# The last pair's V as stationary operand, and a result made in two banks, on two engines, by two queues

**Chip, cores, metric.** One core of one Trainium2 chip. The metric is the device time of one execution in microseconds (us), median of several runs. A matmul of TensorE has a stationary operand, which is loaded first (LDWEIGHTS in the profile), and a moving one; its result goes to a tile in PSUM, which the program allots in banks. SyncE starts the transfers. The granted clock is the share of TensorE's full clock that it got by the profile.

## The reference

A decode step for four sequences, the sum of an attention block and a feed-forward block over one normalized input:

```python
xn = layernorm(x)                                    # x: [4, 1, 512] bf16
q = xn @ wq                                          # 32 heads of 128
p = softmax(einsum("bhqd,bhkd->bhqk", q, k_cache) * 128 ** -0.5)
o = einsum("bhqk,bhkd->bhqd", p, v_cache)            # caches: [4, 32, 8192, 128] bf16
out = x + o_flat @ wo + (silu(xn @ w_gate) * (xn @ w_up)) @ w_down
```

K and V each have one tile of 2 MiB for each of 128 pairs (head, sequence), 512 MiB in all, read once. There is one query row for each, so all the arithmetic is small beside the reading.

## The kernel before

The loop goes over M = 128 pairs m = 4 h + b. Iteration i treats K of pair i and, LP = 4 iterations later, V of that pair. Loads go into nine slots through SyncE's queue; the last V is loaded in four parts. The parts that the change touches:

```python
psM = ... tile_pool(name="psM", bufs=2, space=PSUM)      # 8 banks in all: psS 2, psO 2, psM 2, psX 1, psY 1
psY = ... tile_pool(name="psY", bufs=1, space=PSUM)
yo_ps = psY.tile([B, D], f32)                            # the result: [4, 512]

def pv_chunk(m, k):        # probabilities stationary (4 columns), V moving (512 columns)
    mm(o_acc[h % 2][b * QB:b * QB + NV, :], pt[h][:, s * NV:(s + 1) * NV, 2 * (b * NTG + g)],
       v_tiles[m][:, k * 512:(k + 1) * 512], start=(k == 0))

def fin_1(h):              # the accumulator of a head, 128 x 512, to SBUF
    nc.scalar.copy(out=o_sb[:], in_=o_acc[h % 2][:])

def fin_2(h):              # fold and turn: o as a column of 128 for each b, f32
    for u in range(NV):
        mm(xps[:], o_sb[:, u * Dh:(u + 1) * Dh], ident_f[:, u:P:QB], start=(u == 0))
    nc.vector.tensor_tensor(out=otn[:, h, :], in0=xps[:], in1=rcp.pop(h)[:], op=ALU.mult)

def wo_mm(h):
    mm(yo_ps[0:B, :], otn[:, h, :], w[:, h % (H // 2), :], start=False)
# ... the loop: 16 pv_chunk for each V; fin_1 after the fourth V of a head, fin_2 one iteration later ...
nc.vector.tensor_copy(out=res[:], in_=yo_ps[0:B, :])
nc.sync.dma_start(out=out_flat[:, :], in_=res[:])
```

`mm` is a helper, so nearly all matmuls carry its line, L74, and are told apart by their tiles: `sps` are scores, `oacc` the products with V, `xps` the folded columns, `yo_ps` the result.

Of the kernel before, what the change touches and what calls it, by code (L numbers as in the profile page):

```python
# [8 lines left out]
dt = mybir.dt  # L9
# [6 lines left out]
def kernel(  # L16
# [13 lines left out]
    nc = tc.nc  # L30
    P = nc.NUM_PARTITIONS

    B, Sq, D = A_x.shape
    _, H, Sk, Dh = A_k_cache.shape
# [5 lines left out]
    M = B * H  # L40
    T = Sk // P
    QB = 32
    NQ = P // QB
    TG = 16
    NTG = T // TG
# [10 lines left out]
    out_flat = out.flatten_outer_dims()  # L56
# [5 lines left out]
    persist = ctx.enter_context(tc.tile_pool(name="persist", bufs=1))  # L62
# [2 lines left out]
    small = ctx.enter_context(tc.tile_pool(name="small", bufs=2))  # L65
    psS = ctx.enter_context(tc.tile_pool(name="psS", bufs=2, space=bass.MemoryType.PSUM))
    psO = ctx.enter_context(tc.tile_pool(name="psO", bufs=1, space=bass.MemoryType.PSUM))
    psM = ctx.enter_context(tc.tile_pool(name="psM", bufs=2, space=bass.MemoryType.PSUM))
    psX = ctx.enter_context(tc.tile_pool(name="psX", bufs=1, space=bass.MemoryType.PSUM))
    psY = ctx.enter_context(tc.tile_pool(name="psY", bufs=1, space=bass.MemoryType.PSUM))  # L70
    ctx.enter_context(tc.manual_schedule())

    def mm(out_ap, lhsT, rhs, start, **kw):
        nc.tensor.matmul(out_ap, lhsT=lhsT, rhs=rhs, start=start, stop=True,  # L74
                         skip_group_check=True, **kw)
# [16 lines left out]
    k_tiles, v_tiles = {}, {}  # L92

    def load_k(m):
        h, b = divmod(m, B)
        t_ = slot()
        nc.sync.dma_start(out=t_[:], in_=A_k_cache[b, h, :, :].rearrange("(p t) d -> p (t d)", p=P))  # L97
        k_tiles[m] = t_

    def load_v(m, parts=1):  # L100
        h, b = divmod(m, B)
        t_ = slot()
        src = A_v_cache[b, h, :, :].rearrange("(p t) d -> p (t d)", p=P)
        w = SLOT // parts
        for i in range(parts):
            nc.sync.dma_start(out=t_[:, i * w:(i + 1) * w], in_=src[:, i * w:(i + 1) * w])
        v_tiles[m] = t_
# [7 lines left out]
    ident_f = const.tile([P, P], dt.float32, name="ident_f")  # L115
# [67 lines left out]
    for half in range(NH):  # L183
        for par in range(2):
            for x in range(8):
                mm(qt_ps[:, half, par, x, :], q_bf[:, half, par, x, :, :], pick,
                   start=(half == 0 and par == 0 and x == 0))
# [2 lines left out]

    yfx = persist.tile([B, D], dt.float32, name="yfx")
    otn = persist.tile([P, H, B], dt.bfloat16, name="otn")
    yo_ps = psY.tile([B, D], dt.float32, name="yo_ps")
    ffn = {}

    def load_ffn():
        wg_t, wu_t, wd_t = slot(), slot(), slot()
        w = EC * F
        nc.sync.dma_start(out=wg_t[:, 0:w], in_=B_w_gate.rearrange("(p c) f -> p (c f)", c=EC))
        nc.sync.dma_start(out=wu_t[:, 0:w], in_=B_w_up.rearrange("(p c) f -> p (c f)", c=EC))  # L200
        nc.sync.dma_start(out=wd_t[:, 0:FC * D], in_=B_w_down.rearrange("(p c) e -> p (c e)", c=FC))
        ffn["w"] = (wg_t[:, 0:w].rearrange("p (c f) -> p c f", c=EC),
                    wu_t[:, 0:w].rearrange("p (c f) -> p c f", c=EC),
                    wd_t[:, 0:FC * D].rearrange("p (c e) -> p c e", c=FC))

    def do_ffn():
        wg, wu, wd = ffn["w"]

        gu_ps = psM.tile([P, 2, FC * B], dt.float32, name="mps")
        for i, w in enumerate((wg, wu)):  # L210
            for fc in range(FC):
                for c in range(EC):
                    mm(gu_ps[:, i, fc * B:(fc + 1) * B], w[:, c, fc:F:FC], xnt_w[:, c, 0:B],
                       start=(i == 0 and fc == 0 and c == 0))
        eg = persist.tile([P, FC * B], dt.float32, name="eg")
        nc.scalar.activation(out=eg[:], in_=gu_ps[:, 0, :], func=ACT.Exp, scale=-1.0)
        nc.vector.tensor_scalar(out=eg[:], in0=eg[:], scalar1=1.0, scalar2=None, op0=ALU.add)
        sig = persist.tile([P, FC * B], dt.float32, name="sig")
        nc.vector.reciprocal(out=sig[:], in_=eg[:])
        gs = persist.tile([P, FC * B], dt.float32, name="gs")  # L220
        nc.vector.tensor_tensor(out=gs[:], in0=gu_ps[:, 0, :], in1=sig[:], op=ALU.mult)
        ht = persist.tile([P, FC * B], dt.bfloat16, name="ht")
        nc.vector.tensor_tensor(out=ht[:], in0=gs[:], in1=gu_ps[:, 1, :], op=ALU.mult)
        yf_ps = psM.tile([B, D], dt.float32, name="mps")
        for fc in range(FC):
            mm(yf_ps[0:B, :], ht[:, fc * B:(fc + 1) * B], wd[:, fc, :], start=(fc == 0))
        nc.vector.tensor_tensor(out=yfx[:], in0=yf_ps[0:B, :], in1=xf[:], op=ALU.add)  # L227

        mm(yo_ps[0:B, :], ident_f[0:B, 0:B], yfx[:], start=True)

    wo_t = []

    def load_wo(half):
        n = H // 2
        t_ = slot()
        nc.sync.dma_start(out=t_[:].rearrange("p (h e) -> p h e", h=n),
                          in_=A_wo[half * n * P:(half + 1) * n * P, :].rearrange("(h p) e -> p h e", p=P))
        wo_t.append(t_)


    kts, s_ps, pt, rcp, nmx, osb = {}, {}, {}, {}, {}, {}
# [9 lines left out]
    def t_piece(m, g):  # L251

        w = TG * Dh
        kt = kt_pool.tile([P, w], dt.bfloat16, name="kt")
        src = k_tiles[m][:, g * w:(g + 1) * w].bitcast(dt.uint32)
        nc.vector.transpose(out=kt[:].bitcast(dt.uint32).rearrange("p (j t r) -> p t j r", j=2, r=QB),  # L256
                            in_=src.rearrange("p (t j r) -> p t j r", j=2, r=QB))
        kts[m, g] = kt
# [11 lines left out]
    def max_1(h):  # L270
        mx = small.tile([P, 1], dt.float32, name="mx")
        nc.vector.reduce_max(out=mx[:], in_=s_ps[h][:], axis=AX.X)  # L272
        nmx[h] = mx
# [19 lines left out]
    def pt_turn(h):  # L293
        t_ = pp.tile([P, TG, QB], dt.bfloat16, name="pt_")
        nc.vector.transpose(out=t_[:].rearrange("p t x -> p (t x)"), in_=pt[h][:])
        pt[h] = t_
# [16 lines left out]
        nc.scalar.copy(out=o_sb[:], in_=o_acc[h % 2][:])  # L313
        osb[h] = o_sb

    def fin_2(h):

        o_sb = osb.pop(h)
        xps = psX.tile([P, B], dt.float32, name="xps")
        for u in range(NV):  # L320
            mm(xps[:], o_sb[:, u * Dh:(u + 1) * Dh], ident_f[:, u:P:QB], start=(u == 0))
        nc.vector.tensor_tensor(out=otn[:, h, :], in0=xps[:], in1=rcp.pop(h)[:], op=ALU.mult)  # L322

    def wo_mm(h):
        w = wo_t[h // (H // 2)][:].rearrange("p (h e) -> p h e", e=D)
        mm(yo_ps[0:B, :], otn[:, h, :], w[:, h % (H // 2), :], start=False)

    NK = T // NV
    R_FFN, R_WO = 8, M - 10
    wo_next, wo_ready = 0, 0  # L330
    build_q(0)
    for i in range(M + LP + 1):

        if i + 2 < M:
            load_k(i + 2)
        if 0 <= i + 2 - LP < M:
            load_v(i + 2 - LP, parts=4 if i + 2 - LP == M - 1 else 1)
        if i == R_FFN - 3:
            load_ffn()
        if i == R_FFN:  # L340
            do_ffn()
        if i == R_WO - 3:
            load_wo(0)
        if i == R_WO - 2:
            load_wo(1)
        hs, bs = divmod(i, B)
        hp = hs - 1
        if i < M:
            for g in range(NTG):
                t_piece(i, g)  # L350
                s_piece(i, g)
                if g == 0 and bs == 0 and hp >= 0:
                    pt_turn(hp)
            if bs == B - 2 and hs + 1 < H:
                build_q(hs + 1)
            if bs == B - 1:
                max_1(hs)
        elif i == M:
            pt_turn(H - 1)
        mp = i - LP  # L360
        if 0 <= mp < M:
            for k in range(NK):
                pv_chunk(mp, k)
                if k == NK // 2 and i < M and bs == B - 1:
                    max_2(hs)
            hv, bv = divmod(mp, B)
            if bv == 0:
                row_sums(hv)
            if bv == B - 1:
                fin_1(hv)  # L370
        elif i < M and bs == B - 1:
            max_2(hs)
        mf = i - LP - 1
        if 0 <= mf < M and mf % B == B - 1:
            fin_2(mf // B)
            wo_ready = mf // B + 1
        if i >= R_WO:
            for _ in range(5):
                if wo_next < wo_ready:
                    wo_mm(wo_next)  # L380
                    wo_next += 1
# [2 lines left out]
        wo_next += 1  # L384
    assert wo_next == H

    res = persist.tile([B, D], dt.bfloat16, name="res")
    nc.vector.tensor_copy(out=res[:], in_=yo_ps[0:B, :])  # L388
    nc.sync.dma_start(out=out_flat[:, :], in_=res[:])


# [28 lines left out]
```

## Time and profile before

| | before |
|---|---|
| time, median of the first 3 runs | 1297.76 us (1297.59 to 1297.80) |
| span in the trace | 1295.92 us |
| read from HBM | 550.77 MB, 425 GB/s over the span |
| DMA queue's share of the 16 engines | 99.6% |
| last V but one landed | 1284.17 us |
| from there to the end | 11.75 us |

The table is read from below: nearly everything is transfer, and what compute can change is the last row. The prediction shows the lines.

### The profile page before, as it was taken

The page shows a single profiled execution, that of the slowest core. Times are in us where ns is not written, and L with a number is a line of the kernel's source. Part 1 is how long each engine was busy: PE and PEld are TensorE (multiplying, and loading weights), DVE is VectorE, ACT ScalarE, POOL GpSimd, SP SyncE. Part 2 cuts the span into 40 slices and gives each one's busy share as a digit, 9 for nine tenths or more (in the row PEclk, how much of TensorE's full clock was granted, in tenths as well). Part 3 has the DMA queues.
Part 4 walks back from the last instruction along what each step waited for, and adds up shares of the span by engine and source line. Part 5 has one row for each costly group of instructions (what it writes and reads, how often), then busy time and mean ns, then how long its engine had stood idle before and what let it go on. Part 6 is the DMA issues. An engine that isn't in the chain of part 4 may idle for free.

```text
span 1295.9 us, 11245 instructions
## 1 busy us (share of the span) xinstructions
PE 1095.1 (85%) x4676; PEld 423.2 (33%) x4676; DVE 693.3 (54%) x887; ACT 48.5 (4%) x102; POOL 5.6 (0%) x11
## 2 busy tenths in 40 slices
PE   5889888888888888888888888888888888886987
PEld 2343333333333333333333333333333333332333
DVE  7635554554554565555565455555555555544542
ACT  1000000000000000000000000000000000000000
POOL 1000000000000000000000000000000000000000
PEclk8989999999999999999999999999989989998999
DMA  9999999999999999999999999999999999999997
GB/s 396 429 430 432 431 429 431 431 431 430 430 432 430 430 430 431 431 429 432 432 428 429 434 430 429 431 431 431 431 431 431 430 430 431 430 403 419 432 429 305
DMA packets 42210, 551.49 MB, mean 426 GB/s; under 512 B 4264, under 2 KB 8368, under 8 KB 8880
## 3 DMA queue, kind: packets, MB, share of 16 engines
q1 hardware_dynamic: 42160, 550.79, 99.6%
q8 instruction: 36, 0.59, 0.2%
q14 instruction: 14, 0.11, 0.0%
HBM read 550.77 MB, written 0.00 MB: 425 GB/s over the span
## 4 chain that ended last, share of the span: by engine, by line
DMA 91%; PE 5%; DVE 3%; issue 0%; SPq 0%; ACT 0%; DVEq 0%; ACTq 0%
DMA slot<-in_A_k_cache_dram 86%; DMA slot<-in_B_w_up_dram 3%; DVE kt L256 3%; DMA slot<-in_A_v_cache_dram 3%; PE oacc L74 2%; PE sps L74 2%; PE mps L74 1%; PE xps L74 0%; SPq L97 0%; PE mps L278 0%; SPq L89 0%; DVE mx L272 0%; DVE res L388 0%; DVE yfx L227 0%; ACT o_sb L313 0%
## 5 line engine op out<-in xcount | busy, mean ns | idle before, releaser
L256 DVE STREAM_TRANSPOSE kt<-slot 128x1024 uint32<-128x1024 uint32 x512 | 593.5, 1212 | 284.8 <-DMA slot<-in_A_k_cache_dram 284.8
L74 PE MATMUL sps<-kt,zq 128*128 128x512 bf16 x2048 | 572.1, 416 | 179.0 <-DVE kt L256 165.6
L74 PEld LDWEIGHTS <-zq 128*128 128x128 bf16 x2048 | 208.8, 103 | 532.0 <-issue 361.4
L302 DVE RECIPROCAL rcp<-mps 128x4 f32<-128x4 f32 x32 | 5.8, 183 | 160.9 <-PE mps L74 160.9
L272 DVE TENSOR_REDUCE mx<-sps 128x1 f32<-128x512 f32 x32 | 22.1, 692 | 45.1 <-PE sps L74 45.1
L281 DVE TENSOR_REDUCE nm<-mps 128x4 f32<-128x64 f32 x32 | 7.2, 225 | 50.0 <-PE mps L278 50.0
L74 PE MATMUL xps<-ident_f,o_sb 128*128 128x4 f32 x256 | 33.1, 253 | 0.7 <-ACT o_sb L313 0.7
L74 PEld LDWEIGHTS xps<-ident_f,o_sb 128*128 128x128 f32 x256 | 31.1, 192 | 1.2 <-ACT o_sb L313 1.2
L247 DVE COPY zq<-qt 32x16 bf16<-32x16 bf16 x128 | 23.5, 183 | 1.3
L322 DVE TENSOR_TENSOR otn<-xps,rcp 128x4 bf16<-128x4 f32 x32 | 5.2, 162 | 34.1 <-PE xps L74 34.1
L313 ACT COPY o_sb<-oacc 128x512 f32<-128x512 f32 x32 | 18.7, 585 | 20.6 <-PE oacc L74 20.5
L74 PE MATMUL oacc<-slot,pt__1952 128*4 128x512 bf16 x64 | 14.6, 379 | 0.0
L74 PE MATMUL oacc<-slot,pt__3394 128*4 128x512 bf16 x64 | 14.6, 379 | 0.0
L74 PE MATMUL oacc<-slot,pt__6498 128*4 128x512 bf16 x64 | 14.6, 379 | 0.0
L74 PE MATMUL oacc<-slot,pt__922 128*4 128x512 bf16 x64 | 14.6, 379 | 0.0
L74 PE MATMUL oacc<-slot,pt__2158 128*4 128x512 bf16 x64 | 14.6, 379 | 0.0
L74 PE MATMUL oacc<-slot,pt__3188 128*4 128x512 bf16 x64 | 14.6, 379 | 0.0
L74 PE MATMUL oacc<-slot,pt__4424 128*4 128x512 bf16 x64 | 14.6, 379 | 0.0
L74 PE MATMUL oacc<-slot,pt__5248 128*4 128x512 bf16 x64 | 14.6, 379 | 0.0
L74 PE MATMUL oacc<-slot,pt__6282 128*4 128x512 bf16 x64 | 14.6, 379 | 0.0
L74 PE MATMUL oacc<-slot,pt__371 128*4 128x512 bf16 x64 | 14.6, 379 | 0.0
L74 PE MATMUL oacc<-slot,pt__1128 128*4 128x512 bf16 x64 | 14.6, 379 | 0.0
(204 smaller groups left out, 636.8 us busy)
## 6 DMA issues: line engine op xcount, KB each, us to landing
slot<-in_A_k_cache_dram SPq DMA_DIRECT2D x128, 2048.0 KB, 38.4
slot<-in_A_v_cache_dram SPq DMA_DIRECT2D x127, 2048.0 KB, 38.8
slot<-in_A_wq_dram SPq DMA_DIRECT2D x2, 2048.0 KB, 9.4
slot<-in_A_wo_dram SPq DMA_DIRECT2D x2, 2048.0 KB, 28.8
slot<-in_A_v_cache_dram SPq DMA_DIRECT2D x4, 512.0 KB, 28.0
slot<-in_B_w_gate_dram SPq DMA_DIRECT2D x1, 1792.0 KB, 38.2
slot<-in_B_w_up_dram SPq DMA_DIRECT2D x1, 1792.0 KB
slot<-in_B_w_down_dram SPq DMA_DIRECT2D x1, 1792.0 KB, 34.0
```

The source lines that it names most:

```text
L74: nc.tensor.matmul(out_ap, lhsT=lhsT, rhs=rhs, start=start, stop=True, skip_group_check=True, **kw)
L247: nc.vector.tensor_copy(out=zq[h % 2][a * QB:(a + 1) * QB, :, :, XO + a * QB].rearrange("p b (j r) -> p r j b", r=2), in_=qt[a * QB:(a + 1 ...
L256: nc.vector.transpose(out=kt[:].bitcast(dt.uint32).rearrange("p (j t r) -> p t j r", j=2, r=QB), in_=src.rearrange("p (t j r) -> p t j r", ...
L272: nc.vector.reduce_max(out=mx[:], in_=s_ps[h][:], axis=AX.X)
L281: nc.vector.tensor_reduce(out=nm[:], in_=mps[:, 0:P].rearrange("p (a x g r) -> p x a g r", a=NQ, x=B, r=2)[:, :, :, :, 0], axis=AX.XY, op= ...
L302: nc.vector.reciprocal(out=r_[:], in_=mps[:, P:P + B])
L313: nc.scalar.copy(out=o_sb[:], in_=o_acc[h % 2][:])
L322: nc.vector.tensor_tensor(out=otn[:, h, :], in0=xps[:], in1=rcp.pop(h)[:], op=ALU.mult)
```

## The change

The intent is to shorten what follows the last transfers. For the last pair, V becomes the stationary operand: 64 pieces of 128 x 128 are loaded into the array and each is multiplied by one column of probabilities. (Below, "the 64 pairs" are these 64 weight loads, each with its matmul; "V 126" is V of the (head, sequence) pair 126.) So its o comes out as a column of `xps` at once, and the accumulator's copy and the fold are done for the other three sequences while V still arrives. The result is made in two banks so that two engines can cast it at the same time, and each half has its own store. The second bank comes out of `psM`, and with one `psM` buffer the feed-forward part must run an iteration later.

```diff
-    psM bufs=2 ... psY bufs=1
+    psM bufs=1 ... psY bufs=2
-    yo_ps = psY.tile([B, D], ...)
+    yo_ps = [psY.tile([B, DH], ...) for _ in range(2)]          # DH = 256; all matmuls into it: two of 256 columns
-    R_FFN, R_WO = 8, M - 10
+    R_FFN, R_WO = 9, M - 10
+    def fin_2(h, nb=B):                                         # folds the first nb columns, returns xps
+    def pv_last(xps):
+        h, b = divmod(M - 1, B)
+        for t in range(T):
+            g, u = divmod(t, TG)
+            mm(xps[:, b:b + 1], v_tiles[M - 1][:, t * Dh:(t + 1) * Dh],
+               pt[h][:, u, 2 * (b * NTG + g):2 * (b * NTG + g) + 1], start=False)
...
-        if 0 <= mp < M:
+        if mp == M - 1:
+            xps = fin_2(H - 1, B - 1)
+            pv_last(xps)
+            fin_3(H - 1, xps)                                   # the scaling that fin_2 did before
+            wo_ready = H
+        elif 0 <= mp < M:
...
-            if bv == B - 1:
+            if bv == B - 1 or mp == M - 2:
                 fin_1(hv)
...
-    nc.vector.tensor_copy(out=res[:], in_=yo_ps[0:B, :])
-    nc.sync.dma_start(out=out_flat[:, :], in_=res[:])
+    nc.vector.tensor_copy(out=res[0][:], in_=yo_ps[0][0:B, :])
+    nc.sync.dma_start(out=out_flat[:, 0:DH], in_=res[0][:])
+    nc.scalar.copy(out=res[1][:], in_=yo_ps[1][0:B, :])
+    nc.scalar.dma_start(out=out_flat[:, DH:D], in_=res[1][:])
```

## The prediction

> **What bounds the kernel now.** I first read the page's part on the DMA queues and the head of the chain that ended last, to learn whether an engine or the transfers set the 1297.76 us.
>
> ```profile
> DMA  9999999999999999999999999999999999999997
> q1 hardware_dynamic: 42160, 550.79, 99.6%
> DMA 91%; PE 5%; DVE 3%; issue 0%; SPq 0%; ACT 0%; DVEq 0%; ACTq 0%
> ```
>
> All 40 slices but the last are full of transfer, one queue keeps the 16 DMA engines busy for 99.6% of the span, and 91% of the chain is DMA. The kernel reads 550.77 MB at about 430 GB/s and nothing in the diff removes a byte of it. The TensorE's 85% busy is no bound: it waits for K and V. So only two short stretches can change the time: the start, before the transfers run full (untouched by the change), and the end, after the last of them lands. I therefore read the chain, in order of time, from 1280 us on (start, duration, what).
>
> ```profile
> 1251.39 32.78 DMA slot<-in_A_v_cache_dram
> 1284.17 0.04 issue
> 1284.21 6.23 PE oacc L74 x32
> ...
> 1290.52 0.59 ACT o_sb L313
> ...
> 1291.16 1.07 PE xps L74 x8
> ...
> 1292.25 0.17 DVE otn L322
> ...
> 1292.47 0.39 PE yo_ps L74
> ...
> 1292.88 0.68 DVE res L388
> ```
>
> The chain leaves DMA at 1284.17 us, and 11.75 us of compute and storing follow until 1295.92. The x32 is two V tiles of 16 matmuls each: V of index 126 and the last one, 127, which comes in four parts. To see whether the last part or the TensorE's backlog sets the 32, I read windows of 1 us (busy of each engine, clock, DMA share, GB/s).
>
> ```profile
> 1287.00:1288.00 1.00, 1.00 (x10) 0.45 (x7) 0.00 (x0) 0.00 (x0) 0.00 (x0) 1.00 0.32 131
> 1288.00:1289.00 1.00, 1.00 (x7) 0.38 (x5) 0.00 (x0) 0.00 (x0) 0.00 (x0) 1.00 0.10 41
> 1289.00:1290.00 1.00, 1.00 (x6) 0.41 (x5) 0.00 (x0) 0.00 (x0) 0.00 (x0) 1.00 0.00 0
> ```
>
> The last bytes are there just after 1289.0, while the TensorE is busy without a break until 1290.44: it works off a backlog that began when V 126 landed at 1284.17. The end is a chain that hangs on V 126's landing, at full granted clock, not on the last part.
>
> Then I looked for a row that is like the new matmuls (a whole 128x128 bf16 stationary, a few moving columns). The timeline has two:
>
> ```profile
> 17.17 0.76 PE L74 MATMUL mps<-ident,slot 128*128 128x16 bf16 x24 [0.77 <-DVE slot L177]
> 77.65 3.52 PE L74 MATMUL mps<-xnt_w,slot 128*128 128x4 bf16 x56
> ```
>
> The first, with stationary columns next to each other, takes (0.76 - 0.17) / 23 = 0.0257 us from start to start, where 0.17 is one matmul's own duration (its row on the page: 170 ns). The second, whose stationary columns lie 14 elements apart, takes (3.52 - 0.20) / 55 = 0.060. V's slices are contiguous, so the first is the model.
>
> **What the Trainium skill says.** "TensorE: Matmul & The Clock Gate", section "Single matmul latency", gives (398 + N) / 2.4 ns warm: 379 for N = 512, and the trace has 379; so 272 for the new 256-column matmuls is an estimate from a formula that this trace supports. The same page, "Wait — 56ns, not 53.3ns?", states a start-to-start floor of about 25 ns for small matmuls, which the 0.0257 agrees with; it also says that without hardware decode the sequencer takes about 62 ns for a MATMUL. The 24 in a row above don't show it, but they are fewer than the 64 pairs to come, so no row here excludes it. "PSUM — Partial Sum Buffer", section on bank collisions, says two engines must not be in one bank and 32 partitions at a time: hence the two banks for the result, and nothing in this trace tests that. "DMA: Bandwidth & Descriptors", "Issuing engines are not separate DMA queues", says that two issuing engines save only issue time; the issue of the output took 0.29 us here, and before it nothing else waits on that queue.
>
> **The change part by part.**
> (a) The last V no longer passes through oacc. Its 16 matmuls of 512 columns, 16 x 0.216 = 3.46 us of moving columns, become 64 pairs at 0.0257 = 1.6 us. In the old trace the first four of V 127 ran beside the last of V 126, being in another column group (6.23 us for 32, where 31 x 0.216 + 0.38 would be 7.07), so only about 2.6 us of V 127 was on the path.
> (b) The copy of oacc (0.585 us) and the fold in f32 (eight passes, 1.07 us) move ahead of V 127, to right behind V 126. They are not shortened and, because the fold stands ahead of the 64 in TensorE's program order, they stay on the path; TensorE idles some 0.7 us for the copy.
> (c) The result: the Wo matmul of 512 columns becomes two of 256, the cast of 512 is shared by VectorE and ScalarE, and two queues store halves.
> (d) One psM buffer instead of two, the FFN an iteration later, 32 more Wo matmuls of half the width, one more small f32 matmul: all under the transfers. max_2 fills the one buffer in iteration 4h + 3 and row_sums frees it in 4h + 4; the FFN at iteration 9 finds it free. The FFN weights hold three slots as long as before. I give this zero, with an uncertainty of 0.2 us.
>
> The new end, step by step from V 126 at 1284.21 (old durations and gaps used):
> - its 16 matmuls: 15 x 0.216 + 0.38 = 3.62, done 1287.83;
> - to ScalarE 0.09 (old: 1290.43 to 1290.52), copy 0.585, to TensorE 0.05: 1288.56;
> - eight f32 passes until the next can start, 0.80 + 0.11: 1289.47, after the last part has landed, so no wait for it;
> - 64 pairs: 63 x 0.0257 + 0.17 = 1.79: 1291.26;
> - to VectorE 0.04, the scaling of otn 0.16, to TensorE 0.055: 1291.51;
> - two matmuls of 256 columns: the first done at +0.27, 1291.78, the second 0.11 later, 1291.89;
> - VectorE's cast. Old: 0.679 for 512 and 1.219 for 1024 columns (page rows), so 1.05 ns per column and 0.14 fixed; 256 take 0.41: 1291.82 to 1292.23. ScalarE's copy: 0.585 for 512 and 1.015 for 1024, so 0.84 ns a column and 0.155 fixed; 256 take 0.37: from 1291.98 to 1292.35;
> - the later store is issued by ScalarE at about 1292.4. Old: from the issue at 1293.59 to the end 1295.92, 2.33 us. New end: 1294.73.
>
> Gain: 1295.92 - 1294.73 = 1.2 us. Of it the result's part (c) gives some 0.35: 0.27 on the cast, 0.1 on the first half's start, less what ScalarE's later start takes; the order of V 127 gives the rest, 0.85 to 0.9. 1297.76 - 1.2 = 1296.6 us.
>
> **The rivals.**
> 1. The sequencer, not the array, paces the 64 pairs. If they went at 0.06 us, as the FFN's 56 do, they would take 63 x 0.06 + 0.2 = 4.0 instead of 1.8 and the end would move to 1296.9 on the trace's clock, 1.0 us behind the old: 1298.8 us. For it: nothing here shows more than 24 fast pairs in a row. Against it: the FFN's rate has a cause of its own, its weight loads take 160 ns against 96 of the contiguous ones. I give it 12%.
> 2. The second queue costs more than it saves. ScalarE's queue is used for the first time at the very end, and the program must wait for two stores. If its store took 0.5 to 1 us longer than SP's, the gain would shrink to between 0.7 and 0.2: 1297.1 to 1297.6. Nothing in the trace of before shows that queue at all, which is why I can't exclude it.
> 3. The transfers carry the change of (d): a slot freed later by the moved FFN or by the single psM buffer opens a gap in the queue. Each load waits some 38 us from issue to landing, so a delay of two or three us in freeing a slot is hidden; the FFN's stretch (60 to 100 us) has no gap in before although VectorE stood still 8.5 us for it. I expect nothing; a gap of 1 us would eat the gain.
> 4. The gain is larger: if the two V tiles' landings lay closer in this run, or the loads of V 127 ran ahead of the fold, the floor is the last part's landing, about 1289.1; that would be 1295.2. Program order speaks against it.
>
> **Range and chances.** The three old runs lie within 0.21 us, so noise is small; the spread comes from rivals 1 and 2. Centre 1296.6, range 1295.8 to 1297.9. Two per cent are 26 us, over twice the whole stretch after V 126's landing (11.75 us). So even the loss of everything there gives no "faster", and "slower" needs a gap in the transfers that I see no reason for: faster 0.003, within 0.989, slower 0.008.
>
> **What would show it.** In the new profile: the same 99.6% or so on the queue and the same GB/s in the slices; the chain's last DMA piece still V, ending near 1284, then 16 oacc matmuls (not 32), the copy, eight passes, then 64 matmuls on xps within about 1.8 us; a cast of about 0.41 on VectorE beside a copy of 0.37 on ScalarE that overlap; two output stores, the ends within 0.2 us of each other, and about 2.3 us from the later issue to the end. I am wrong if the 64 take over 2.5 us, if from the last issue to the end it is over 2.8 us, or if the chain's last DMA piece ends over 0.5 us later than 1284.17.

## The result, and the profile after

1296.49 us (1296.41 to 1296.67, 6 runs) against 1297.78 us (1297.59 to 1297.96, 6 runs) of the kernel before: 1.29 us less, ratio 0.9990, 95% interval 0.9977 to 1.0003. A ratio is the mean time of one kernel's fast runs over that of the other's of the same rounds, so not quite the ratio of the medians quoted. By the 2% rule the verdict is "same"; the runs of the two kernels do not overlap, though.

The page after, DMA shares of the slices and queues (packets, MB, share of the 16 engines):

```profile
DMA  9999999999999999999999999999999999999997
q1 hardware_dynamic: 42160, 550.79, 99.7%
q10 hardware_dynamic: 8, 0.00, 0.0%
```

The transfers are what they were. The one new line is ScalarE's queue, with the eight packets of its half of the output. The chain of the changed kernel from 1280 us on (start, duration, what):

```profile
1284.17 0.04 issue
1284.21 3.63 PE oacc L74 x16
...
1287.92 0.59 ACT o_sb L316
...
1288.56 2.67 PE xps L74 x72
...
1291.25 0.17 DVE otn L328
...
1291.46 0.39 PE yo_ps L74 x2
...
1291.88 0.36 ACT res L410
```

V 126 landed at 1284.17, in both traces. Behind it stand 16 matmuls on `oacc` instead of 32 (3.63 us against 6.23), and 72 on `xps` instead of 8 (2.67 against 1.07): 2.60 saved, 1.60 spent. The timeline of the same stretch has the new rows (start, duration, engine, instruction, what it waited for):

```profile
1289.47 1.74 PE L74 MATMUL xps<-pt__6945,slot 128*128 128x1 bf16 x64
1291.77 0.41 DVE L408 CAST res<-yo_ps 4x256 bf16<-4x256 f32 x1 [0.36 <-PE yo_ps L74]
1291.88 0.36 ACT L410 CAST res<-yo_ps 4x256 bf16<-4x256 f32 x1 [3.38 <-PE yo_ps L74]
1292.21 0.29 SPq L409 DMA_DIRECT2D out_dram<-res  x1
1292.27 0.56 ACTq L411 DMA_DIRECT2D out_dram<-res  x1
```

The two casts overlap. ScalarE's issue takes 0.56 us, SyncE's 0.29, and the span ends at 1294.65, 2.38 us after the later one.

### The profile page after: what moved, and what is told of

It is laid out like the page before. It is cut to its first block, busy times and chain, and to the rows that moved or that the text cites. A ratio compares the mean times of both kernels' runs of the same rounds, so it can differ in the third digit from the quotient of the medians.

```text
span 1294.7 us, 11411 instructions
## 1 busy us (share of the span) xinstructions
PE 1091.8 (84%) x4758; PEld 425.8 (33%) x4758; DVE 693.1 (54%) x887; ACT 48.9 (4%) x103; POOL 5.6 (0%) x11
## 3 DMA queue, kind: packets, MB, share of 16 engines
q1 hardware_dynamic: 42160, 550.79, 99.7%
## 4 chain that ended last, share of the span: by engine, by line
DMA 89%; PE 8%; DVE 3%; issue 0%; SPq 0%; ACT 0%; DVEq 0%; ACTq 0%
DMA slot<-in_A_k_cache_dram 86%; PE sps L74 4%; PE oacc L74 3%; DMA slot<-in_A_v_cache_dram 3%; DVE kt L259 3%; PE xps L74 0%; SPq L97 0%; PE mps L281 0%; PE mps L74 0%; SPq L89 0%; DVE otn L328 0%; ACT o_sb L316 0%; DVE pt__4838 L298 0%; DVE pt__6510 L298 0%; DVE pt__4014 L298 0%
## 5 line engine op out<-in xcount | busy, mean ns | idle before, releaser
L74 PE MATMUL xps<-ident_f,o_sb 128*128 128x4 f32 (+1 forms) x256 | 33.1, 253 | 0.7 <-ACT o_sb L316 0.7
```

What stands on the lines that cost most here:

```text
L74: nc.tensor.matmul(out_ap, lhsT=lhsT, rhs=rhs, start=start, stop=True, skip_group_check=True, **kw)
```

## The experiments

The diffs are shortened. All were timed in five rounds; the runs of each group shared a chip and the runs of the kernel before. "Less" or "more" is the difference of medians to that kernel before. Two compute something wrong. All twelve passed the comparison with the reference, those two as well: one column of one head weighs too little in the result for its tolerance, so the comparison proves little of the last head, and that the changed kernel itself, e7, e8, e10 and e11 are right there rests on their code.

| run | median us (range) | before us | difference | ratio, 95% interval |
|---|---|---|---|---|
| e1_v_order_only | 1297.04 (1296.63 to 1297.07) | 1297.80 | -0.76 | 0.9993, 0.9981 to 1.0006 |
| e2_result_only | 1297.53 (1297.40 to 1297.65) | 1297.80 | -0.27 | 0.9998, 0.9984 to 1.0012 |
| e3_buffers_only | 1297.82 (1297.76 to 1298.09) | 1297.80 | +0.02 | 1.0000, 0.9988 to 1.0013 |
| e4_pairs_twice | 1298.29 (1298.22 to 1298.38) | 1297.80 | +0.49 | 1.0004, 0.9991 to 1.0016 |
| e5_one_queue | 1296.68 (1296.62 to 1296.79) | 1297.69 | -1.01 | 0.9992, 0.9979 to 1.0004 |
| e6_one_store | 1296.58 (1296.30 to 1296.81) | 1297.69 | -1.11 | 0.9991, 0.9979 to 1.0004 |
| e7_parts_before_fold | 1295.76 (1295.56 to 1295.80) | 1297.69 | -1.93 | 0.9984, 0.9971 to 0.9998 |
| e8_whole_head | 1295.10 (1295.05 to 1295.20) | 1297.69 | -2.59 | 0.9980, 0.9967 to 0.9992 |
| e9_strided_v | 1298.81 (1298.74 to 1298.94) | 1297.69 | +1.12 | 1.0009, 0.9996 to 1.0021 |
| e10_keep_warm | 1295.25 (1295.06 to 1299.68) | 1297.69 | -2.44 | 0.9992, 0.9980 to 1.0005 |
| e11_eight_parts | 1294.90 (1294.87 to 1295.01) | 1297.69 | -2.79 | 0.9978, 0.9966 to 0.9991 |
| e12_after_again | 1296.63 (1296.45 to 1296.76) | 1297.69 | -1.06 | 0.9991, 0.9978 to 1.0005 |

The intervals of the ratios are wider than most of these differences, so I lean on the traces, and on the ranges of the runs, for anything under 1 us.

### The change taken apart

**e1_v_order_only**: the last V's new way, the result as before.

```diff
 # the changed kernel, with
-    psM bufs=1, psY bufs=2, yo_ps in two banks, two casts, two stores, R_FFN = 9
+    psM bufs=2, psY bufs=1, yo_ps in one bank, one cast, one store, R_FFN = 8
```

> Only the last V's new way (stationary, behind the fold); the result in one bank, one cast, one store, two psM buffers, FFN at iteration 8, as before. My theory (the two parts add): the 64 pairs end near 1291.2 us, then one Wo matmul of 512 columns (0.38), a cast of 0.68 on VectorE, issue near 1292.6, end near 1294.9 in the trace: 1.0 us under the kernel before, 1296.8 us. Rival A (the gain is the result's): within 0.2 us of before. Rival B (the gain is the moved FFN or the single psM buffer, that is, in the transfers): within 0.2 us of before and the last V landing at the old place.

0.76 us less, where 1.0 was expected. Its timeline shows what took the difference:

```profile
1289.58 1.77 PE L74 MATMUL xps<-pt__6913,slot 128*128 128x1 bf16 x64
1291.61 0.59 PE L74 MATMUL yo_ps<-slot,otn 128*4 128x512 bf16 x1 [0.26 <-DVE otn L326]
```

The pairs go as predicted; the Wo matmul of 512 columns took 0.59 us, in the trace before 0.38. In this run the granted clock had fallen to half at 1290.76. In the profile the end came at 1295.27 where 1294.9 was expected, 0.37 late: 0.21 of it is this matmul, and 0.12 is V 126, which landed at 1284.29 instead of 1284.17. For the other timed runs the clock at that moment is not on record, so that it explains the missing 0.24 there too is likely, not shown. Rivals A and B fall: most of the gain is here, and the landing was not earlier.

**e2_result_only**: the kernel before with the result in two banks, two casts and two stores (and the buffers and the FFN's place that this asks for).

```diff
 # the kernel before, with
+    psM bufs=1, psY bufs=2, yo_ps in two banks, two casts, two stores, R_FFN = 9
```

> Only the result in two banks, two casts, two stores (with the single psM buffer and the FFN at iteration 9 that the banks ask for); the last V as before. My theory: the later store is issued near 1293.27 instead of 1293.59, and the end is 0.27 us under the kernel before: 1297.5 us. Rival A: 1.2 us under it, 1296.5. A second queue that costs would show as 0 or slower.

0.27 us less, as expected. Rival A (the whole gain is the result's) falls.

**e3_buffers_only**

```diff
 # the kernel before, with
-    psM bufs=2 ... R_FFN, R_WO = 8, M - 10
+    psM bufs=1 ... R_FFN, R_WO = 9, M - 10
```

> Only the single psM buffer and the FFN at iteration 9. My theory: under the transfers, so 0 within 0.15 us of the kernel before, with the last V landing within 0.1 us of 1284.17 in the trace. Rival B: 1 us or more faster or slower.

0.02 us more: nothing in time. In its one profiled run V 126 landed at 1284.57, 0.4 later than in the trace before, more than the 0.1 I had expected; the changed kernel, with the same two edits, has 1284.17 in one profile and 1284.45 in another (e12), so this is scatter between runs. Rival B falls.

The parts add to 0.76 + 0.27 = 1.03 us; the whole took 1.29 less in its first six runs and 1.06 (e12) beside the last group.

**e4_pairs_twice**: each of the 64 pairs is done twice. The result is wrong.

```diff
-        for t in range(T):
+        for t in [t_ for t_ in range(T) for _ in range(2)]:
```

> The changed kernel with each of the 64 pairs done twice: the last column comes out double (wrong on purpose). If the 64 are on the path and paced at 25 ns, 128 of them take 64 x 0.025 = 1.60 us more: 1298.1 us. If a queue[...] had hidden a slower sequencer[...], the second half would show it: start to start over 25 ns in the trace and up to 4 us more. If the 64 are hidden: no change.

```profile
1289.57 3.44 PE L74 MATMUL xps<-pt__6945,slot 128*128 128x1 bf16 x128
1293.27 0.58 PE L74 MATMUL yo_ps<-slot,otn 128*4 128x256 bf16 x2 [0.25 <-DVE otn L328]
```

128 pairs take 3.44 us, (3.44 - 0.16) / 127 = 0.0258 from start to start. By the trace's single rows the first 64 go at 25.0 ns; the granted clock fell to half at 1291.31, and the last 48, all behind that, go at 26.7. So the second half is 7% slower, with the clock, and nothing near 60 ns shows up. The time is 1.78 us over the changed kernel when each is taken against its own before (+0.49 against -1.29), or 1.55 against e12 (+0.49 against -1.06); 1.60 was expected. The 64 pairs are on the path in full.

**e9_strided_v**: stationary columns 14 elements apart, the FFN's stride. The result is wrong.

```diff
-            mm(xps[:, b:b + 1], v_tiles[M - 1][:, t * Dh:(t + 1) * Dh], ...
+            mm(xps[:, b:b + 1], v_tiles[M - 1][:, t * 100:t * 100 + FC * Dh:FC], ...
```

> The changed kernel with the stationary columns 14 elements apart, as in the FFN (wrong on purpose: other columns of V). My theory (the FFN's 60 ns a pair comes from its strided weight loads): 64 pairs at 0.060, 4.0 us instead of 1.8, and 1298.7 us, 2.2 over the changed kernel. Rival (the FFN's pace was the sequencer's or the FFN's own): the pace stays at 25 ns and the time at 1296.5.

```profile
1289.45 3.99 PE L74 MATMUL xps<-pt__6945,slot 128*128 128x1 bf16 x64
```

3.99 us and 2.18 us more than e12 on the same chip: 0.060 a pair, the FFN's pace to the digit. So the choice of row in the prediction (contiguous columns as the model, not the FFN's) was right for the reason given: the stride of the stationary operand makes the difference.

### The stores

**e5_one_queue**

```diff
-    nc.scalar.dma_start(out=out_flat[:, DH:D], in_=res[1][:])
+    nc.sync.dma_start(out=out_flat[:, DH:D], in_=res[1][:])
```

> The changed kernel with both halves stored by SyncE's queue. My theory: the first half is issued while ScalarE still copies, the second right after the copy, at the same 1292.3 or at most 0.25 us later (behind the first issue of 0.29): 0 to 0.25 us over the changed kernel, 1296.5 to 1296.75. Rival (the second queue is worth its issue time or more): 0.3 us or more over it. Rival 2 (the second queue costs): under it by 0.1 or more.

**e6_one_store**

```diff
-    res: two tiles of [B, DH], each with its store
+    res: one tile of [B, D]; both casts write into it, then
+    nc.sync.dma_start(out=out_flat[:, :], in_=res[:])
```

> The changed kernel with both casts into one tile and one store by SyncE, issued when both are done. My theory: issue near 1292.27, the end as in the changed kernel within 0.1 us. Rival: the two stores save something, then 0.2 us or more over it.

The timeline of e5 and then of e6, from the Wo matmuls on:

```profile
1291.41 0.59 PE L74 MATMUL yo_ps<-slot,otn 128*4 128x256 bf16 x2 [0.26 <-DVE otn L328]
1292.03 0.36 ACT L410 CAST res<-yo_ps 4x256 bf16<-4x256 f32 x1 [3.67 <-PE yo_ps L74]
1292.26 0.29 SPq L409 DMA_DIRECT2D out_dram<-res  x1
1292.65 0.28 SPq L411 DMA_DIRECT2D out_dram<-res  x1
```

```profile
1291.53 0.59 PE L74 MATMUL yo_ps<-slot,otn 128*4 128x256 bf16 x2 [0.25 <-DVE otn L328]
1292.15 0.36 ACT L409 CAST res<-yo_ps 4x256 bf16<-4x256 f32 x1 [3.63 <-PE yo_ps L74]
1292.54 0.29 SPq L410 DMA_DIRECT2D out_dram<-res  x1
```

Measured from the end of ScalarE's cast to the end of the span, the three ways take 2.41 us (two queues, from 1292.24 to 1294.65), 2.45 (one queue, two stores, to 1294.84) and 2.37 (one store, to 1294.88). That is the same within 0.08 us. But e5 and e6 have the Wo matmuls at half clock, and with two queues at half clock (e4, e8, e9) the stretch took 2.32: like with like, the second queue may be worth 0.05 to 0.13 us of a profile. In time e5 is 0.05 us over and e6 0.05 us under e12 (whose group had the same 1297.69 before), and they are 0.19 and 0.09 over the first runs of the changed kernel; the half clock at the Wo matmuls (0.59 instead of 0.38) is as much. So in the times the second queue, and even the second store, earn nothing that can be told from scatter. What part (c) gains comes from the two banks and two casts: each engine casts 256 columns, and VectorE starts 0.31 us after the first Wo matmul does instead of 0.41.

### Who holds the end

**e7_parts_before_fold**: three parts of the last V ahead of the fold.

```diff
-            xps = fin_2(H - 1, B - 1)
-            pv_last(xps)
+            xps = psX.tile([P, B], dt.float32, name="xps")
+            pv_last(xps, 0, 3 * T // 4)          # the first of these has start=True
+            fin_2(H - 1, B - 1, xps)
+            pv_last(xps, 3 * T // 4, T)
```

> The changed kernel with three of the last V's four parts (48 pairs) ahead of the fold, the last 16 pairs behind it. My theory (the path hangs on V 126: matmuls, copy, fold, and the 64 stand behind them though TensorE idles): the 48 fill TensorE's idle 0.7 us during the copy; 48 x 0.025 = 1.2 from 1287.67, fold 0.9, 16 x 0.025 = 0.4: done near 1290.35 instead of 1291.21: 0.85 us under the changed kernel, 1295.65. Rival (the landing of the last part, near 1289.1, sets the end): no gain.

```profile
1287.83 1.35 PE L74 MATMUL xps<-pt__6945,slot 128*128 128x1 bf16 x48
1287.99 0.59 ACT L316 COPY o_sb<-oacc 128x512 f32<-128x512 f32 x1 [12.76 <-PE oacc L74]
1289.04 1.03 PE L74 MATMUL xps<-ident_f,o_sb 128*128 128x3 f32 x8
1289.94 0.54 PE L74 MATMUL xps<-pt__6945,slot 128*128 128x1 bf16 x16
```

1.93 us less than before, 0.87 less than e12 (expected 0.85). The 48 pairs run beside the copy, in what was idle time of the TensorE. Same work, other order: the order had cost it.

**e8_whole_head**: all four V of the last head stationary; no accumulator, no copy, no fold for that head.

```diff
+    def pv_col(m):                                # 64 pairs into column b of xps
+        mm(xps[:, b:b + 1], v_tiles[m][:, t * Dh:(t + 1) * Dh], pt[h][...], start=(b == 0 and t == 0))
-        if mp == M - 1:
+        if M - B <= mp < M:
+            if mp == M - B: fin_3(H - 2, fin_2(H - 2)); wo_ready = H - 1     # xps has one buffer
+            pv_col(mp)
```

> The changed kernel with all four V of the last head as stationary operand: no oacc, no copy, no fold for that head. My theory: V 126 is done at 1284.2 + 1.8, TensorE waits for the last part, which lands near 1289.13, and 16 pairs (0.4) follow: done near 1289.7 instead of 1291.21: 1.5 us under the changed kernel, 1295.0. If less comes, the last part lands later than I read from the DMA share.

```profile
1284.24 2.29 PE L74 MATMUL xps<-pt__6945,slot 128*128 128x1 bf16 x80 [3.03 <-DMA slot<-in_A_v_cache_dram]
1286.71 0.58 PE L74 MATMUL xps<-pt__6945,slot 128*128 128x1 bf16 x16 [0.18 <-DMA slot<-in_A_v_cache_dram]
1288.01 0.59 PE L74 MATMUL xps<-pt__6945,slot 128*128 128x1 bf16 x16 [0.71 <-DMA slot<-in_A_v_cache_dram]
1289.19 0.59 PE L74 MATMUL xps<-pt__6945,slot 128*128 128x1 bf16 x16 [0.60 <-DMA slot<-in_A_v_cache_dram]
1290.04 0.59 PE L74 MATMUL yo_ps<-slot,otn 128*4 128x256 bf16 x2 [0.26 <-DVE otn L328]
```

2.59 us less than before, 1.53 less than e12 (expected 1.5). Now the TensorE waits for each part, and the end hangs on the last landing, 1289.15. The clock was granted half from 1279.4 on, and the 80 pairs still went at (2.29 - 0.17) / 79 = 0.027. The Wo matmuls did pay: 0.59 instead of 0.38.

**e10_keep_warm**: e8 with 24 matmuls of 512 columns into an unused bank, to hold the clock (and `row_sums` of the last head ahead of its first pairs).

```diff
+            n_ = {(0, 63): 8, (1, 63): 8, (2, 63): 4, (3, 31): 2, (3, 47): 2}.get((b, t), 0)
+            for _ in range(n_): mm(d_[:], ident[:], v_tiles[m - 1][:, 0:512], start=True)
```

> The whole-head kernel with 24 matmuls of 512 columns into an unused bank, in TensorE's idle time between the V tiles and parts of the last head (none behind the last part). In the trace of the whole-head kernel the clock was granted half from 1279.4 us on, and its two Wo matmuls took 0.59 instead of 0.38. My theory: the 64-pair stretches count as idle for the clock; kept warm, the Wo matmuls take 0.38 again and the time falls by 0.2 us, to 1294.9. Rival: the fill is in the way of the last part (0.2 us or more over), or the half clock costs nothing (same).

No gain: three runs at 1295.06 to 1295.25 and two at 1298.56 and 1299.68. The timeline of the profiled run, which is one of the good kind:

```profile
1289.37 0.54 PE L74 MATMUL xps<-pt__6945,slot 128*128 128x1 bf16 x16
1290.16 0.38 PE L74 MATMUL yo_ps<-slot,otn 128*4 128x256 bf16 x2 [0.25 <-DVE otn L328]
```

The clock came back to full at 1280.74, in the fill, and held to 1290.98; the Wo matmuls took 0.38 again. The fill also closed TensorE's idle time, so this run alone doesn't tell which of the two did it. e9 does in part: there TensorE's rows have no gap from 1288.54 on (the fold, then pairs), and the clock fell to half all the same at 1291.97, 3.4 us later. So the pairs did not hold the clock there, busy or not. The fill of e10, however, put the last 16 pairs to 1289.37, 0.18 later than in e8, and from ScalarE's cast to the end this profile took 2.42 us against 2.32: nothing is left of the 0.21. The two slow runs have no profile; a fill at half clock, twice as long and in the way, would do it, but that stays open.

**e11_eight_parts**: e8 with the last V in eight parts.

```diff
-            load_v(i + 2 - LP, parts=4 if i + 2 - LP == M - 1 else 1)
+            load_v(i + 2 - LP, parts=8 if i + 2 - LP == M - 1 else 1)
```

> The whole-head kernel with the last V loaded in eight parts instead of four. My theory: behind the last landing stand 8 pairs instead of 16: 8 x 0.026 = 0.2 us less, 1294.9, if the last landing stays near 1289.15. Rival: eight smaller transfers land later (0.2 us or more), no gain.

1294.90, 0.20 under e8, and the best of all: 1.73 us under e12 of the same chip and rounds, 2.79 under the kernel before. The number is as expected, but the profile doesn't show it coming from where it was expected:

```profile
1289.44 0.38 PE L74 MATMUL xps<-pt__6945,slot 128*128 128x1 bf16 x8 [0.26 <-DMA slot<-in_A_v_cache_dram]
1290.07 0.59 PE L74 MATMUL yo_ps<-slot,otn 128*4 128x256 bf16 x2 [0.26 <-DVE otn L328]
1290.69 0.36 ACT L420 CAST res<-yo_ps 4x256 bf16<-4x256 f32 x1 [15.44 <-PE yo_ps L74]
```

The last part landed at 1289.39, not near 1289.15 (V 126 was 0.08 later as well; SyncE issued the last part only at 1284.30). So the pairs were done at 1289.82, in e8 at 1289.78, and ScalarE's cast ended 0.03 later than in e8. The span is 0.22 shorter, though, as from that cast to the end it took 2.07 us instead of 2.32. The stores landed at 1292.26 in e8 and 1292.29 in e11. SyncE then ends the program with five checks of semaphores, 0.06 us apart. In e8 the stores' semaphores stand in the first two checks, so all five follow the landing, to 1292.56; in e11, with four more transfers issued, they stand in the third and the fifth, so only the fifth follows it, to 1292.34. From the last check to the end all fourteen profiles have 0.79. So in this profile the gain comes from the order of the closing checks and not from fewer pairs behind the landing; that it has the expected size is luck. The other four runs of e11 have no profile.

**e12_after_again**: the changed kernel, unchanged.

> The changed kernel once more, beside the others on one chip, to compare with: 1296.5 us. If the run to run spread of 0.26 us is the clock at the Wo matmuls, its trace shows them at 0.38 or 0.59.

1296.63. V 126 landed at 1284.45 in its profile, 0.28 later than in the first, and the Wo matmuls took 0.38: the 0.28 us by which this profile's span is longer is the transfers' scatter and not the clock. So the clock's 0.2 us is not the whole of the scatter between runs.

## Why the prediction was right

1296.6 was predicted, with 1295.8 to 1297.9; 1296.49 and 1296.63 were measured. Step by step, the prediction's number first and the trace's behind it:

- The chain hangs on V 126's landing: 1284.17 and 1284.17. Its 16 matmuls done: 1287.83 and 1287.84. The copy's end and the fold's start: 1288.56 and 1288.56. The 64 pairs' start: 1289.47 and 1289.47. These steps only moved rows that the old trace already had, with their gaps, and so they hit to a hundredth.
- The 64 pairs: 1.79 us and 1.74. This was the one real choice, between two rows with paces of 26 and 60 ns. e9 shows that the choice was right for its reason, e4 that the 64 lie on the path and that no limit shows up to 128.
- VectorE's cast 0.41 and 0.41, ScalarE's 0.37 and 0.36: straight lines through two widths held down to 256.
- From the later issue to the end: 2.33 and 2.38. End: 1294.73 and 1294.65. Small misses cancel in part here: the pairs were 0.05 faster, ScalarE began its cast 0.02 us after the Wo matmuls and not 0.09, and what follows the issue took 0.05 more.
- Where the gain came from: 0.85 to 0.9 for the order of V 127 and 0.35 for the result was predicted. The chain gives 2.60 - 1.60 = 1.0 for the order, and e2 gives 0.27 for the result. So the stated split leaned too far to the result by about 0.1. It is a slip in the sum and not in the mechanism: the prediction's own steps move the Wo matmul from 1292.47 to 1291.51, which is 0.96 for the order, and leave 0.23 for the result. (e1 measured 0.76 for the order in time, with the Wo matmul at half clock in its profile.) In e2 the stretch from the Wo matmul to the last issue shrank by 0.31 (1293.59 - 1292.47 before, 1293.31 - 1292.50 in e2), and 0.05 of it was lost after the issue.
- Part (d), nothing: e3 has +0.02.

The rivals: the first (the sequencer paces the pairs) is refuted by the 128 pairs at 25 to 27 ns. The second (the new queue costs 0.5 us or more) is refuted; it gives nothing that shows in the times, and costs little. Its issue is longer, 0.56 us, but from the issue's start to the store's landing it took 1.30 us, SyncE's 1.18 in the same profile: 0.12 more, not 0.5. The third (a gap in the transfers) is refuted by e3 and by the queue's 99.7%. The fourth named 1295.2 as what the end would be if the last part's landing set it. It did not come by itself, as program order had the fold in the way; e8 took that away and got 1295.1. How the prediction came to 1295.2 it doesn't show, so that the two are this close may be luck.

Not foreseen was the clock. The pairs did not hold it (e4, e9), and depending on when it fell the Wo matmuls took 0.38 or 0.59 us; it was full in both profiles of the changed kernel and half in those of e1, e4, e5, e6, e8, e9 and e11.

## What to carry to other kernels

When transfers fill the whole span, only the chain behind the last landing is left to win. Write it out with the trace's own rows and gaps, and ask of each piece whether it must stand behind the landing or can run before it; here the order of work (e7, e8) was worth more than splitting the last cast, and a second store queue was worth nothing that the times show. A gain of the expected size is not yet the expected gain: look in the profile where it came from (e11). For a new instruction, look for a row of the same shape in the same trace, and check that the layout of its operands is the same too: a strided stationary operand made it 2.3 times slower.

## What the Trainium skill lacked or had wrong

- "TensorE: Matmul & The Clock Gate", "Wait — 56ns, not 53.3ns?": its floor of about 25 ns between starts agrees (64 pairs of weight load and matmul at 25.0 ns), and its 62 ns for a decode by the sequencer did not bind here. Lacking: the pace of pairs with one column at half clock, 26.7 ns (e4, e8), only 7% slower, while a 512-column Wo matmul went from 0.38 to 0.59 us (e1).
- Same page, "Weight-path perf modes": it gives the range of column steps in which the fast weight load applies, but that section has no cost of a step. 14 elements apart, a pair took 60 ns instead of 26 (e9, and the FFN's 56 pairs).
- Same page, on the clock gate: it tells of keeping the TensorE busy, not what counts as busy. In e9 the matmul rows covered all 3.41 us up to the fall to half at 1291.97, as a fold in f32 and pairs with one moving column; in e10 512-column matmuls brought the clock back to full at 1280.74.
- "DMA: Bandwidth & Descriptors", "Issuing engines are not separate DMA queues": it holds. That section has no figure for the issue itself: 0.56 us on ScalarE against 0.29 on SyncE for 2 KB, but from the issue's start to the store's landing 1.30 against 1.18 (changed kernel), and 1.20 against 1.18 where the two issues began 0.16 us apart and not 0.06 (e8).
- On none of the pages: the program ends with SyncE's checks of five pairs of semaphores, 0.06 us apart, and how many of them stood behind the last store's landing changed the span by 0.22 us (e11 against e8).
